# Moving the six weight conversions of the first attention stage one pair later, and holding ScalarE's first step of each in its place

## The chip, the cores and the metric

One core of one Trainium2 chip. The metric is the device time of one execution in microseconds (us), the median over runs. Engines by their short names: PE (TensorE, matrix products), PEld (its weight loads), ACT (ScalarE), DVE (VectorE), POOL (GpSimd), SP (SyncE, which issues the transfers here).

## The reference

Three stages of one network, all in float32:

```python
scores = q @ k.T / sqrt(64); scores[masked] = -1e9          # 4 x 12 heads, 448 x 64, causal
attn   = softmax(scores) @ v
x      = attn as (1792, 768)                                 # tokens by heads x width
h      = x @ w_in                                            # 768 x 2048, w_in is float64 in memory
x      = max(0.01 * h, h) @ w_out                            # 2048 x 768, float64 too
logits = x @ phi                                             # 32 slots
out    = softmax(logits, 1) @ experts(softmax(logits, 0).T @ x)   # 8 experts, w1 and w2
```

The float64 inputs of this step are turned into narrower numbers on the chip; that is what the text calls a conversion.

## The kernel before

**Attention** goes by pairs of heads: 6 pairs for each of the 4 batches, 24 in all, numbered n. It is a generator (L587) whose every step is called a slot, three slots to a pair. For n up to 6, slot 0 of pair n is `attend(n-1)` (the product with v, tile `O`), `lowering(n)` (tiles `mps`, `mr`) and `weights(n, 0)` (scores `T`, then the exponential into `P`); slot 1 is `inverses(n-1)` (tile `dn`, then a reciprocal `r` on DVE), maxima of pair n+1 (scores `S`, DVE's `junk`) and `weights(n, 1)`; slot 2 is `columns(n-1)` (tiles `rb`, `rs`, `x`), `weights(n, 2)`, more maxima and the transposes `qkps`, `qkt` of pair n+2. In `weights` POOL masks `P` (L481) and adds up `tsum` (L486, L490), which `inverses` reads.

**The first stage** (`stage(SLOTS * NP + LEAD, EARLY[0])`, L902) has 21 slots, numbered x: pairs 0 to 6 of attention, and in between six conversions of `w_in`, f = 0 to 5. The loop of `stage` (L873 to L882) takes one slot of attention, then `prep_step(BEFORE)`, then starts conversions that are due, then `prep_step(AFTER)`. Where they are due is a ramp: up to `ceil(6 * (x + 1) / 17)` are started by slot x, which gives slots 0, 2, 5, 8, 11, 14.

**A conversion** (`prep_in`, L242) has three parts. In its starting slot s (`to_f32`, L219): ACT takes the absolute value of the high words (L230, tile `cv_i`, `t` in the code), ACT takes their sign (L231, tile `cs_i`), DVE a maximum (`w_am`, L233), a shift (L234) and an or (L235) that puts the low words in; then `load_raw` issues the transfer that is due next into the freed buffer. At the end of slot s+1 `pow2_scale` (L137) makes a scale: one product on PE (`w_ps`) and short steps on DVE (`w_m`, `w_e`, `w_s`). In slot s+2 ACT scales the sign, POOL multiplies it in (L254), ACT copies the high half (`w`, L262; for f = 0 and 4 POOL does that, L260), POOL subtracts for the low half (L263). Raw tiles have 3 buffers, `cv_i` 4, `cs_i` 2 in this stage.

**The order of the work.** PE's products run in the order in which the program states them (`in_order`, L102). On the other engines a planner sets the order: it goes through a simulated time line and gives an engine whatever is ready by it, attention ahead by a priority offset (`AHEAD`, 300). `tc.issue_after(i)` holds an instruction behind i in its engine's queue, without waiting for i to finish. From the second stage on (`fixed[0] = True`, L910) ACT is in program order as well; in the first it is not. Transfers are all on SP's queue; the raw tiles are issued behind the last load of attention (`last_load`, L195).

**The second stage** begins with pair 7; from here PE also runs the large product `H` of the batch before (18 products for each of 16 columns of `w_in`), which needs all six `x` of its batch and the converted `w` of its column. Its own pool of raw tiles lies in the memory of the first stage's, which it gets tile by tile as that comes free.

Of the kernel before, what the change touches and what calls it, by code (L numbers as in the profile page):

```python
# [10 lines left out]
F32 = mybir.dt.float32  # L11
# [4 lines left out]
AF = mybir.ActivationFunctionType  # L16
# [18 lines left out]
def tile_attn_moe_softmoe(ctx: ExitStack, tc: tile.TileContext, q, k, v, w_in, w_out, phi, w1, w2, out, dbg=None):  # L35
# [60 lines left out]
    def last_on(engine):  # L96
        return next(i for i in reversed(nc.cur_bb.bb.instructions[-400:]) if i.engine == engine)
# [21 lines left out]
    scalar = Scalar()  # L119
# [56 lines left out]
    for x, u in enumerate(units):  # L176
        stage = 0 if x < EARLY[0] else 1 if x < whole else 2
        order += [u + (h, stage) for h in ((0, 1) if stage == 2 else (None,))]
# [5 lines left out]
    def load_raw():  # L184

        while waiting:
            u = waiting[0]
            kind, f, h, stage = u
            pool, n = pools[stage], BUFS[stage][0]
            if pool is None or sum(x[3] == stage for x in raws) == n:  # L190
                return
            waiting.pop(0)
            w = DM if h is None else DH
            t = pool.tile([128, w, 2], I32, tag="raw", bufs=n, name=f"raw_{kind}{f}_{h}")
            with tc.issue_after(last_load[0]):  # L195
                if kind == "i":
                    nc.sync.dma_start(
                        t.rearrange("p (c f) t -> p c (f t)", f=128),
                        w_in32[:, 256 * f : 256 * (f + 1)].rearrange("(c p) f -> p c f", p=128),
                    )  # L200
                else:
                    g0, ng = 2 * (h or 0), w // (DM // 4)
                    rows = w_out32[128 * f + 32 * g0 : 128 * f + 32 * (g0 + ng)].rearrange("(g p) c -> p g c", p=32)
                    for e in range(4):
                        with tc.issue_after(last_on(mybir.EngineType.SP)) if e else ExitStack():
                            nc.sync.dma_start(
                                t[32 * e : 32 * e + 32].rearrange("p (g c) t -> p g (c t)", g=ng),
                                rows[:, :, DM // 2 * e : DM // 2 * (e + 1)],
                            )
            raws[u] = t  # L210
# [8 lines left out]
    def to_f32(u, absmax=None):  # L219

        raw = raws.pop(u)
        kind, f, h, stage = u
        nm = f"{kind}{f}_{h}"
        w = DM if h is None else DH
        hw, lw = raw[..., 1], raw[..., 0]
        _, nt, ns = BUFS[stage]
        t = pools[stage].tile([128, w], F32, tag="cv_t", bufs=nt, name="cv_" + nm)
        sg = pools[stage].tile([128, w], BF16, tag="cv_s", bufs=ns, name="cs_" + nm)
        ti = t.bitcast(I32)
        scalar.activation(t, hw.bitcast(F32), AF.Abs, scale=2.0**-112)  # L230
        scalar.activation(sg, hw.bitcast(F32), AF.Sign)  # L231
        if absmax is not None:
            nc.vector.tensor_reduce(absmax, t, AX.X, ALU.max)  # L233
        nc.vector.tensor_scalar(ti, ti, 3, None, ALU.logical_shift_left)  # L234
        nc.vector.scalar_tensor_tensor(ti, lw, 29, ti, ALU.logical_shift_right, ALU.bitwise_or)  # L235
        load_raw()
        return t, sg
# [4 lines left out]
    def prep_in(u):  # L242

        f = u[1]
        am = const.tile([128, 1], F32, tag="w_am", bufs=2, name=f"w_am{f}")
        t, sg = to_f32(u, am)
        yield AFTER
        yield AFTER
        s_w, _ = pow2_scale(am, f"w{f}", 20, out=inv_w[:, f : f + 1])
        yield BEFORE  # L250
        if u[3]:
            yield BEFORE
        scalar.activation(sg, sg, AF.Copy, scale=s_w)
        nc.gpsimd.tensor_tensor(t, t, sg, ALU.mult)  # L254
        if u[3]:
            yield BEFORE
        w = t.rearrange("p (c f) -> p c f", c=NP)
        hi, lo = (w16[f][:, x] for x in range(2))
        if f < EARLY[0] and f % 4 < HIP:
            nc.gpsimd.tensor_copy(hi, w)  # L260
        else:
            scalar.copy(hi, w)  # L262
        nc.gpsimd.tensor_tensor(lo, w, hi, ALU.subtract)  # L263
        ready.add(u[:2])

    def prep_out(us):
# [5 lines left out]
        for u in us:  # L272
            wo, sg = to_f32(u)
            nc.gpsimd.tensor_tensor(wo, wo, sg, ALU.mult)  # L274
            wo = wo.rearrange("p (g c) -> p g c", c=DM // 4)
            g0, ng = 2 * (u[2] or 0), wo.shape[1]
            for e in range(4):
                with tc.issue_after(last_on(mybir.EngineType.SP)) if e else ExitStack():
                    nc.sync.dma_start(
                        rows[:, g0 : g0 + ng, DM // 4 * e : DM // 4 * (e + 1)], wo[32 * e : 32 * e + 32]  # L280
                    )
            wos.append((wo, g0, ng))
            if u is not us[-1]:
                yield BEFORE
# [27 lines left out]
    started = [0]  # L312
    running = []

    def prep_step(phase):

        for x in list(running):
            if x[1] == phase:
                x[1] = next(x[0], None)
                if x[1] is None:  # L320
                    running.remove(x)

    def prep_start():
        u = units[started[0]]
        started[0] += 1
        us = [x for x in order if x[:2] == u]
        g = prep_in(us[0]) if u[0] == "i" else prep_out(us)
        running.append([g, next(g)])
# [540 lines left out]
    def stage(slots, count, columns_of_g=None):  # L869

        had = started[0]
        last = slots - (6 if columns_of_g is not None and count <= NF else 4)
        for x in range(slots):  # L873
            with tc.high_priority(offset=AHEAD):
                next(slots_of_attention, None)
            prep_step(BEFORE)
            while started[0] < min(count, had + -(-(count - had) * (x + 1) // last)):
                prep_start()
            if columns_of_g is not None and x not in GAPS:
                with tc.high_priority(offset=AHEAD):  # L880
                    next(columns_of_g)
            prep_step(AFTER)  # L882
        if columns_of_g is not None:
            with tc.high_priority(offset=AHEAD):
                for _ in columns_of_g:
                    pass
        while running:
            prep_step(BEFORE)
            prep_step(AFTER)

    if True:
# [6 lines left out]
        for e in range(4):  # L898
            nc.sync.dma_start(
                phi_sb[32 * e : 32 * e + 32], phi[DM // 4 * e : DM // 4 * (e + 1)].rearrange("(y x) s -> x y s", x=32)  # L900
            )
        stage(SLOTS * NP + LEAD, EARLY[0])  # L902
        tc_release(pools[0])
        tc_release(psum)
# [6 lines left out]
        for b in range(1, 4):  # L911
            if b == 3:
                tc_release(pools[1])
                tc_release(ring[0])
                mainp = tc.alloc_tile_pool(name="mainp", bufs=1, reuse_waits="tile")
                ring[0] = tc.alloc_tile_pool(name="gring2", bufs=1, reuse_waits="tile")
                pools[2] = tc.alloc_tile_pool(name="conv", bufs=1, side="right", reuse_waits="tile")
                load_raw()
                g_nat = [mainp.tile([128, S // 64, DFF // 4], F32, name=f"g_nat{h}") for h in range(2)]
            stage(SLOTS * NP, sum(EARLY[: b + 1]) if b < 3 else 2 * NF, up(b - 1))  # L920
# [322 lines left out]
```

## Time and profile before

| what | value |
|---|---|
| median of 3 runs | 623.68 us (623.65 to 625.51) |
| the profiled execution, its time | 622.72 us |
| its span, first to last instruction | 621.0 us (1.7 us lie around it) |
| PE busy | 560.4 us, 90% |
| DVE busy | 399.7 us, 64% |
| ACT busy | 277.4 us, 45% |
| POOL busy | 240.7 us, 39% |
| mean granted clock of PE | 0.988 |

Times in the trace are microseconds from the start of the span. The time line lists, for one engine, groups of alike instructions: start, duration, engine, line, operation, tiles, count, and in brackets how long the engine had been idle and what it had waited for. Most of ACT's and PE's lines are those of a helper (L115, L104), so groups are told apart by their tiles. Buffer numbers are left out: `cv_i_None` is the tile of any of the conversions of this stage, and which f it is follows from the order.

### The profile page before, as it was taken

How to read it: one execution, taken by the hardware profiler on the slowest of the kernel's cores; microseconds unless marked ns; L12 is line 12 of the kernel's file. 1: busy time of each engine (PE TensorE's matmuls, PEld its weight loads, DVE VectorE, ACT ScalarE, POOL GpSimd, SP SyncE). 2: the span in 40 equal slices, each digit the busy share in tenths (PEclk: the TensorE clock that was granted, in tenths of full speed). 3: DMA queues.
4: the chain of work that ended last, by engine and by line, in shares of the span. 5: the costliest groups of instructions: out<-in, count | busy, mean ns of one | idle time of the engine just before them, and what ended most of it. 6: DMA issues, size and time to landing. Idle time of an engine off the chain costs nothing.

```text
span 621.0 us, 12409 instructions
## 1 busy us (share of the span) xinstructions
PE 560.4 (90%) x4720; PEld 316.4 (51%) x4720; DVE 399.7 (64%) x970; ACT 277.4 (45%) x538; POOL 240.7 (39%) x247
## 2 busy tenths in 40 slices
PE   4788888997999999899999999999999999996584
PEld 3455555654555555555555555554434444552353
DVE  5988657998984686898779999642866433001014
ACT  2577655678765466556445554431112121001013
POOL 5476973488686372576445443430000000000000
PEclk9989999998999999999999999999999999999998
DMA  9972337754783388895344323219959559999998
GB/s 182 275 166 46 68 74 206 216 155 116 174 179 88 74 213 198 196 201 127 110 109 96 109 78 90 58 60 319 366 223 421 196 210 392 426 417 427 402 334 301
DMA packets 137308, 125.70 MB, mean 202 GB/s; under 512 B 86688, under 2 KB 131232, under 8 KB 133792
## 3 DMA queue, kind: packets, MB, share of 16 engines
q1 hardware_dynamic: 137248, 124.91, 65.6%
q8 instruction: 37, 0.61, 0.4%
q14 instruction: 23, 0.19, 0.1%
HBM read 105.74 MB, written 19.14 MB: 201 GB/s over the span
## 4 chain that ended last, share of the span: by engine, by line
PE 56%; DMA 14%; DVE 10%; POOL 7%; issue 4%; ACT 4%; SPq 3%; DVEq 0%; ACTq 0%; POOLq 0%
PE H L104 26%; DMA w<-in_moe_w_dram 9%; PE O L104 5%; PE T L104 4%; PE g_acc L104 3%; PE dn L104 3%; PE L L104 3%; DMA raw_o_None<-in_moe_w_out_dram 2%; DVE rs L519 2%; PE S L104 2%; POOL w L263 2%; DVE junk L441 2%; DVE cv_i_None L235 2%; DMA raw_i_None<-in_moe_w_in_dram 1%; PE ph L1064 1%
## 5 line engine op out<-in xcount | busy, mean ns | idle before, releaser
L104 PE MATMUL H<-x,w 128*128 128x448 f16 x1152 | 229.9, 354 | 0.7 <-ACT g L115 0.7
L104 PEld LDWEIGHTS <-w 128*128 128x128 f16 x1152 | 110.3, 99 | 112.8 <-issue 19.6
L441 DVE CUSTOM_DVE_ANT_0 junk<-S,mask 112x224 bf16<-112x224 f32 (+3 forms) x192 | 84.1, 438 | 24.1 <-PE S L104 21.5
L115 ACT ACTIVATE P<-T 112x672 f32<-112x672 f32 (+1 forms) x72 | 57.0, 793 | 27.2 <-PE T L104 26.5
L519 DVE RECIPROCAL rs<-rs 128x224 f32<-128x224 f32 x36 | 53.2, 1519 | 19.1 <-ACT rs L115 19.0
L104 PE MATMUL T<-qkt 64*112 64x336 f32 (+3 forms) x576 | 60.6, 322 | 2.6 <-DVE mxe L441 2.5
L481 POOL TENSOR_SCALAR_AFFINE_SELECT P<-P 112x448 f32<-112x448 f32 x48 | 33.2, 695 | 75.8 <-ACT P L115 60.7
L115 ACT ACTIVATE g<-H,iv 128x448 f32<-128x448 f32 x48 | 30.5, 635 | 64.3 <-PE H L104 43.1
L104 PE MATMUL O<-P,v 112*64 112x448 f32 (+3 forms) x384 | 52.4, 413 | 4.5 <-POOL P L481 4.5
L104 PEld LDWEIGHTS T<-qkt 64*112 64x112 f32 x576 | 42.3, 179 | 17.7 <-issue 9.6
L490 POOL TENSOR_TENSOR tsum<-tsum,P 112x448 f32<-112x448 f32 (+1 forms) x48 | 49.4, 1029 | 1.9
L486 POOL TENSOR_TENSOR tsum<-P 112x672 f32<-112x672 f32 x24 | 39.8, 1658 | 1.7
L104 PEld LDWEIGHTS O<-P,v 112*64 112x64 f32 x384 | 25.4, 138 | 29.3 <-issue 12.3
L1056 POOL MEMSET hz<- 128x256 f32 x2 | 0.6, 312 | 100.9 <-PE pgt L104 100.3
L115 ACT ACTIVATE mr<-mps,own 128x112 fp32r<-128x112 f32 x96 | 26.2, 357 | 30.0 <-PE mps L104 30.0
L104 PE MATMUL S<-qkt 64*112 64x224 f32 (+3 forms) x192 | 31.3, 366 | 7.0 <-DVE mxe L441 2.6
L115 ACT ACTIVATE g_spare<-H,iv 128x448 f32<-128x448 f32 x16 | 10.2, 635 | 56.8 <-PE H L104 56.8
L104 PE MATMUL T<-mr,onesr 64*112 64x448 f32 (+1 forms) x192 | 30.6, 315 | 4.1 <-ACT mr L115 4.1
L254 POOL TENSOR_TENSOR cv_i_None<-cv_i_None,cs_i_None 128x768 f32<-128x768 f32 x16 | 28.6, 1786 | 10.5 <-ACT cs_i_None L115 10.5
L263 POOL TENSOR_TENSOR w<-cv_i_None,w 128x768 f16<-128x768 f32 x16 | 26.8, 1676 | 10.4 <-ACT w L115 10.3
L554 POOL TENSOR_TENSOR x<-rs,x 128x448 f16<-128x448 f32 x24 | 26.6, 1107 | 8.1 <-ACT x L115 8.1
L274 POOL TENSOR_TENSOR cv_o_None<-cv_o_None,cs_o_None 128x768 f32<-128x768 f32 x10 | 16.5, 1650 | 33.4 <-DVE cv_o_None L235 21.2
(180 smaller groups left out, 875.6 us busy)
## 6 DMA issues: line engine op xcount, KB each, us to landing
w<-in_moe_w_dram SPq DMA_DIRECT2D x30, 1536.0 KB, 14.6
raw_i_None<-in_moe_w_in_dram SPq DMA_DIRECT2D x16, 768.0 KB, 6.0
raw_o_None<-in_moe_w_out_dram SPq DMA_DIRECT2D x40, 192.0 KB, 4.4
g_far<-g SPq DMA_DIRECT2D x32, 224.0 KB, 2.3
gb<-g_far SPq DMA_DIRECT2D x8, 896.0 KB, 9.0
wo<-wsc SPq DMA_DIRECT2D x4, 1536.0 KB, 9.1
v<-in_v_dram SPq DMA_DIRECT2D x24, 224.0 KB, 4.3
out_dram<-ob SPq DMA_DIRECT2D x14, 384.0 KB, 3.8
```

The lines of the kernel that those rows point to most:

```text
L104: op(*args, **kwargs)
L115: op(*args, **kwargs)
L235: nc.vector.scalar_tensor_tensor(ti, lw, 29, ti, ALU.logical_shift_right, ALU.bitwise_or)
L254: nc.gpsimd.tensor_tensor(t, t, sg, ALU.mult)
L263: nc.gpsimd.tensor_tensor(lo, w, hi, ALU.subtract)
L274: nc.gpsimd.tensor_tensor(wo, wo, sg, ALU.mult)
L441: nc.vector.tensor_tensor_reduce(out=junk[:, :w], in0=ps[:, a, at : at + w], in1=mask[:, S - w :], scale=-1.0, scalar=3e38, op0=ALU.add, o ...
L481: nc.gpsimd.affine_select(out=d, in_=d, compare_op=ALU.is_ge, fill=0.0, base=0, pattern=[[0, 4], [1, CP]], channel_multiplier=-1,)
L486: nc.gpsimd.tensor_tensor(tsum[:CP], p[0][:CP, :, 0, CP:], p[0][:CP, :, 1, : S - CP], ALU.add)
L490: nc.gpsimd.tensor_tensor(y, y, p[1][:CP, :, j, : S - CP * (j + 2)], ALU.add)
L519: nc.vector.reciprocal(rs[:, c : c + S // 2], rs[:, c : c + S // 2])
L554: nc.gpsimd.tensor_tensor(x16[b][:, hp, 1], rs, hi, ALU.subtract)
```

## The change

In the first stage (`columns_of_g is None`) the ramp is replaced by a formula that starts conversions at slots 1, 5, 8, 11, 14 and 17. And in that stage, for f from 1 to 5, ACT's absolute value is held behind the ACT instruction that the program states last before it. The other stages keep their ramp.

```diff
@@ to_f32
-        scalar.activation(t, hw.bitcast(F32), AF.Abs, scale=2.0**-112)
+        with tc.issue_after(last_on(mybir.EngineType.Activation)) if stage == 0 and f else ExitStack():
+            scalar.activation(t, hw.bitcast(F32), AF.Abs, scale=2.0**-112)
         scalar.activation(sg, hw.bitcast(F32), AF.Sign)
@@ stage
-            while started[0] < min(count, had + -(-(count - had) * (x + 1) // last)):
+            if columns_of_g is None:
+                begun = min(x, 1) + max(x - 2, 0) // 3
+            else:
+                begun = had + -(-(count - had) * (x + 1) // last)
+            while started[0] < min(count, begun):
                 prep_start()
```

## Rows read from the trace of the kernel before

**Rows 1.** Busy time by stretch; its first line names the columns.
```profile
core 0: us, PE busy (x) PEld busy (x) DVE busy (x) ACT busy (x) POOL busy (x), PEclk, DMA share, GB/s
26.30:41.20 14.90, 12.19 (x102) 8.32 (x101) 14.41 (x43) 9.72 (x17) 11.01 (x9) 0.89 0.82 208
41.20:52.30 11.10, 9.60 (x102) 6.52 (x101) 8.91 (x30) 8.78 (x17) 8.65 (x9) 1.00 0.28 64
300.00:420.00 120.00, 116.89 (x887) 65.22 (x886) 92.13 (x204) 58.87 (x127) 54.06 (x55) 1.00 0.32 83
520.00:621.00 101.00, 77.57 (x842) 43.15 (x838) 15.08 (x41) 12.94 (x29) 2.84 (x16) 0.97 0.97 386
```

**Rows 2.** ACT's time line: start, length, engine, line, operation, tiles, count, [idle before].
```profile
20.05 0.89 ACT L115 ACTIVATE cv_i_None<-raw_i_None 128x768 f32<-128x768 f32 x1 [2.53 <-DMA raw_i_None<-in_moe_w_in_dram]
...
21.62 0.71 ACT L115 ACTIVATE P<-T 112x672 f32<-112x672 f32 x1
22.31 0.92 ACT L115 ACTIVATE cv_i_None<-raw_i_None 128x768 f32<-128x768 f32 x1
...
25.09 0.93 ACT L115 ACTIVATE cv_i_None<-raw_i_None 128x768 f32<-128x768 f32 x1 [1.05 <-DMA raw_i_None<-in_moe_w_in_dram]
25.92 0.70 ACT L115 ACTIVATE P<-T 112x672 f32<-112x672 f32 x1
```

**Rows 3.** Time line of PE, pairs 0 and 1.
```profile
21.98 0.80 PE L104 MATMUL w_ps<-ident,w_am 128*128 128x128 f32 x2 [2.95 <-DVE w_am L233]
...
24.25 0.48 PE L104 MATMUL S<-qkt 64*112 64x224 f32 x2
...
30.40 0.32 PE L104 MATMUL mps<-ident,mxe 112*128 112x112 f32 x1 [0.83 <-DVE mxe L441]
...
33.59 0.45 PE L104 MATMUL T<-mr,onesr 64*112 64x448 f32 x2 [1.88 <-ACT mr L115]
```

**Rows 4.** Time line of POOL, pairs 1 to 6.
```profile
37.96 0.58 POOL L481 TENSOR_SCALAR_AFFINE_SELECT P<-P 112x448 f32<-112x448 f32 x1 [3.11 <-ACT P L115]
...
49.12 0.60 POOL L481 TENSOR_SCALAR_AFFINE_SELECT P<-P 112x448 f32<-112x448 f32 x1 [2.37 <-ACT P L115]
...
55.64 1.65 POOL L263 TENSOR_TENSOR w<-cv_i_None,w 128x768 f16<-128x768 f32 x1
...
60.27 0.58 POOL L481 TENSOR_SCALAR_AFFINE_SELECT P<-P 112x448 f32<-112x448 f32 x1 [2.37 <-ACT P L115]
...
71.50 0.82 POOL L260 CAST w<-cv_i_None 128x768 f16<-128x768 f32 x1
...
95.54 0.58 POOL L481 TENSOR_SCALAR_AFFINE_SELECT P<-P 112x448 f32<-112x448 f32 x1 [4.70 <-ACT P L115]
...
99.44 1.88 POOL L490 TENSOR_TENSOR tsum<-tsum,P 112x448 f32<-112x448 f32 x2
```

**Rows 5.** Time line of PE, `dn` of pairs 2 and 6.
```profile
57.95 0.41 PE L104 MATMUL dn<-tsum,sixteen 128*64 128x112 f32 x4 [0.51 <-POOL tsum L490]
...
101.84 0.73 PE L104 MATMUL dn<-tsum,onesr 128*64 128x336 f32 x4
```

**Rows 6.** Time line of ACT: a sign in pair 2, the absolute value of f = 8.
```profile
53.81 0.92 ACT L115 ACTIVATE cs_i_None<-raw_i_None 128x768 bf16<-128x768 f32 x1
...
115.50 0.93 ACT L115 ACTIVATE cv_i_None<-raw_i_None 128x768 f32<-128x768 f32 x1
```

**Rows 7.** Time line of DVE, pairs 1 and 3.
```profile
30.26 2.18 DVE L235 SCALAR_TENSOR_TENSOR cv_i_None<-raw_i_None,cv_i_None 128x768 int32<-128x768 int32 x1
...
56.96 0.94 DVE L233 TENSOR_REDUCE w_am<-cv_i_None 128x1 f32<-128x768 f32 x1
...
58.55 0.85 DVE L529 RECIPROCAL r<-dn 128x112 f32<-128x112 f32 x1
59.31 0.90 DVE L235 SCALAR_TENSOR_TENSOR cv_i_None<-raw_i_None,cv_i_None 128x768 int32<-128x768 int32 x1
```

**Rows 8.** Time line of SP, the raw tiles of the second stage.
```profile
90.18 2.79 SPq L197 DMA_DIRECT2D raw_i_None<-in_moe_w_in_dram x3
```

## The prediction

> **What bounds the kernel now.** I read the busy times by stretch first, because the change touches only the first hundred microseconds. From pair 2 of the first stage a pair takes some 11 us, and PE is busy 9.60 of 11.10 at full clock; pair 1 takes 14.90, with 12.19 of PE at a mean clock of 0.89 [rows 1]. So pair 1 has about 4 us that the pairs behind it don't need. Much later, at 300 to 420 us, PE is busy 116.89 of 120: from there the kernel is a chain of products, and a lead that the first stage wins is carried along. The last stretch is full of transfers (DMA share 0.97), but those go into buffers that earlier work frees, so they move with it [rows 1]. I take the whole lead as carried.
>
> Then the time lines of the slow first pairs. On ACT, pair 0's second exponential (tile P) starts at 21.62, behind the absolute value of f = 0, which stood 2.53 us waiting for its transfer. Its third starts at 25.92, behind the absolute values of f = 1 and f = 2, and the latter waited 1.05 us for a landing [rows 2]. By the code these two belong to slots 2 and 5; the planner has drawn them forward, and ACT's queue holds the exponential behind them. PE shows what follows: 2.95 us idle ahead of w_ps, whose maximum DVE had not ready; the next scores S only at 24.25; 0.83 us ahead of mps at 30.40, since DVE still had parts of three conversions to do; and 1.88 us for ACT's mr at 33.59 [rows 3].
>
> Last, POOL for the steady part. It masks P of the pairs at 37.96, 49.12, 60.27 and so on; between the second and third lie 11.15 us, of which POOL is idle 2.37, so it works 8.8 [rows 4]. Its final sum releases dn, for which PE sat 0.51 us [rows 5]. A pair is therefore a loop: POOL's 8.8 us, then some 2.4 us over dn, the scores and the exponential back to POOL. A conversion is 3.3 us of it (two steps of 1.65 [rows 4]).
>
> **The change part by part.** No instruction is added or removed: six conversions move, and five absolute values are held in place.
>
> *Start.* The absolute values of f = 1 and 2 no longer stand ahead of the exponential. It is then bound by the one before it, which ends at 21.62 + 0.71 = 22.33 [rows 2]; the scores S, which need the buffer that this one frees, can start at about 22.4 instead of 24.25: 1.85 us [rows 2, 3]. w_ps of f = 0 moves to the end of slot 2, behind those scores, so PE's idle time ahead of it is part of the same gain. With two conversions gone from DVE and ACT here, the waits of 0.83 and 1.88 go too. Sum 4.56; I take 4.5. Bounds: 1.85 alone, if ACT and DVE stay as late as now; up to 7, if f = 0 too gets behind the exponential (2.53, [rows 2]). It isn't held by the change, so I leave it where it is, at no gain. What is late next is PE itself: pair 1 then has POOL work for f = 0 only, and PE's products set its length.
>
> *The loops from pair 2 to 5.* They now carry f = 1 to 4, one each, as before with other numbers. Before, four loops from 49.12 to 95.54 took 46.42 us, since the planner had drawn two conversions ahead of the mask [rows 4]. Held in place they should go like the one of 11.15, with POOL's copy for f = 4 (0.82, [rows 4]) in one of them: 4 x 11.15 + 0.82 = 45.4, a gain of 1.0. Bounds: 0, if they are drawn ahead again, and 1.8, if the copy falls into POOL's gap.
>
> *Holding the absolute value.* On ACT it should cost nothing: it comes where a sign of 0.92 stands now, at 53.81 [rows 6], and the sign, which is free, can go to where an absolute value of about 0.92 was [rows 2]. Without that exchange mr, behind it, would be 0.9 us late. On DVE it costs: the maximum (0.94), the shift and the or (0.90) of a conversion must now run between ACT's end at 54.7 and the reciprocal r of dn at 58.55, where attention's maxima run too; today the or comes behind r, at 59.31 [rows 6, 7]. Who waits for r is rb on PE, and all products behind it. From both sides: 0 if the planner leaves the or behind r, 0.90 a pair if it comes ahead [rows 7]. I take 0.35, nearer to the lower end, since attention has the better priority: 5 pairs x 0.35 = 1.7 lost.
>
> *The last conversion.* f = 5 moves from pair 5 to pair 6, where POOL now sits 4.70 us before its mask at 95.54 [rows 4]. But the conversion comes behind that mask: the sum of pair 6 ends at 99.44 + 1.88 = 101.32 and PE's dn comes at 101.84, a slack of 0.5 [rows 4, 5]. One step of 1.65 ahead of the sum costs 1.1 us, two cost 2.8; if both are put behind it, nothing. I take 1.4, near to one step.
>
> *Transfers.* The raw tiles of f = 3 to 5 are issued later, as their buffers free up, and have about a pair's time to land (the waits of [rows 2] are those for the first three, whose transfers the change does not touch). On SP the loads of q, k and v stand behind them, and those are due two pairs ahead. The raw tiles of the second stage go out at 90.18 [rows 8]; the third, that of f = 8, now needs memory that f = 5 holds until its last POOL step, near 100. Cover: the conversion of f = 8 begins at 115.50 [rows 6], 15 us later. I cost all this at nothing; without that cover it would be the few microseconds by which f = 5 is late.
>
> **The sum.** -4.5 - 1.0 + 1.7 + 1.4 = -2.4 us. The profiled execution took 622.72 (span 621.0 and 1.7 around it), which gives 620.3. The median of the runs is 0.96 above it, so the forecast of a median is 623.68 - 2.4 = **621.3 us**.
>
> **The rivals.** What a measurement of this kernel can tell from no change is about 0.3%, 1.9 us.
>
> *A, the forecast*: some -1 to -4.
>
> *B, the gain is kept whole.* f = 5 goes behind the sum into POOL's idle time, and DVE's or stays behind r: -4.5 - 1.0 = -5.5, and up to -7.5 if PE's clock also stays up in pair 1. About 618. For it: POOL has gaps in each pair [rows 4]. Against: DVE works 8.91 of 11.10 us in a pair [rows 1], and has to find room for three steps in a shorter stretch.
>
> *C, the change doesn't clear ACT.* Only the absolute value is held. The signs need the same raw tiles and are free; drawn forward to where the absolute values were, they keep the exponential behind a landing. Then the start gives its lower bound: -1.85 - 1.0 + 1.7 + 1.4 = +0.25, 624. For it: the planner fills ACT's idle time with anything ready. Against: there are two sign buffers, and the first stays taken until POOL has multiplied it.
>
> *D, slower: DVE in the first half of each pair.* The or comes ahead of r in pairs 2 to 6, and beside a busy POOL. In the trace the or takes 0.90 at 59.31, where POOL stands in its gap (the 2.37 us ahead of 60.27), and 2.18 at 30.26, where POOL works [rows 4, 7]. Between ACT's end and r POOL is at work, so it would cost between 0.90 and 2.18 a pair, say 1.5: 5 x 1.5 = 7.5 - 4.5 - 1.0 + 1.4 = +3.4, 627. It decides from (4.5 + 1.0 - 1.4) / 5 = 0.8 us a pair on. Against: attention's priority. The Trainium skill has a rule that bears on it: GPSIMD Engine Reference, 1. Specifications, says that POOL and DVE share their interfaces to the on-chip memory, and that DVE instructions with two such inputs contend; the or is one of them. By that rule the change is bad, as it moves these steps from POOL's gaps into its work; the trace agrees with 0.90 against 2.18.
>
> **How the numbers follow.** Chances: A 0.42, B 0.20, C 0.18, D 0.20. Faster by more than 0.3% (below 621.8) is B and somewhat over half of A, 0.48; within it the rest of A, most of C and the mild end of D, 0.32; slower the rest, 0.20. The range must reach into B and D: 617.5 (6.2 gained) to 626.5 (2.8 lost) leaves out the far ends of both, less than 0.2. A's own range is 620 to 622.7.
>
> **What would show it.** Right: on ACT no absolute value but that of f = 0 ahead of pair 0's third exponential, and that at about 22.4; POOL's mask of pair 1 at 33 to 34 instead of 37.96, of pair 2 near 45, of pair 6 near 91 to 92; dn of pair 6 at 99 to 100. A step fails if pair 1's mask is not 4 us earlier (start), if masks stand over 11.5 us apart from pair 2 on with r or w_ps awaited on PE (holding, D), or if PE waits 2 us or more for POOL's sum in pair 6 (last conversion). The forecast is wrong as a whole if the lead at the first H is over 2 us and the end is not earlier.

## The result, and the profile after

The changed kernel took **631.30 us** (median of 4 runs, 630.67 to 632.78) beside 624.11 for the one before (4 runs): a ratio of 1.0101, 95% interval 1.0079 to 1.0124 (ratios here and below are the recorded estimates, which differ a little from the quotient of the two medians, here 1.0115). It is slower by 1.0%; the forecast was 621.3, and even the upper end of its range, 626.5, lies 4.8 us below. The profiled execution took 630.67, its span is 628.9 against 621.0, the mean granted clock 0.977 against 0.988. Of the six conversions five moved by a pair, f = 0 by one slot. The work is the same: PE 565.4 us busy, DVE 401.5, ACT 276.6, POOL 240.6.

Where it went is seen at the head of each pair. Below stands when PE starts the product `O` of each pair (in slot 0 of the next one), in both traces, with the distance to the next:

| `O` of pair | before | distance | after | distance | after against before |
|---|---|---|---|---|---|
| 0 | 26.34 | 14.88 | 24.60 | 10.33 | -1.74 |
| 1 | 41.22 | 11.05 | 34.93 | 10.55 | -6.29 |
| 2 | 52.27 | 10.92 | 45.48 | 16.74 | -6.79 |
| 3 | 63.19 | 10.22 | 62.22 | 11.76 | -0.97 |
| 4 | 73.41 | 11.31 | 73.98 | 15.32 | +0.57 |
| 5 | 84.72 | 14.99 | 89.30 | 15.46 | +4.58 |
| 6 | 99.71 | | 104.76 | | +5.05 |
| first `H` | 102.66 | | 109.39 | | +6.73 |

By pair 3 the change is 6.8 us ahead, more than I had asked of the start. The next four pairs lose 11.8 us, and with another 1.7 behind `O` of pair 6, 6.7 us of loss are left at the first `H`. From there it is only carried: a block of `H` that starts at 480.34 before starts at 487.09 now.

The busy times by stretch, profile after (the answer to [rows 1]; the columns are the same):

```profile
24.60:34.90 10.30, 10.11 (x100) 6.72 (x99) 6.71 (x30) 5.67 (x12) 8.92 (x9) 1.00 0.79 169
34.90:45.50 10.60, 9.46 (x103) 6.35 (x101) 8.46 (x29) 6.89 (x14) 5.57 (x6) 1.00 0.53 141
45.50:62.20 16.70, 11.40 (x99) 7.71 (x99) 10.84 (x31) 10.08 (x19) 11.53 (x10) 0.86 0.35 90
62.20:74.00 11.80, 10.28 (x102) 6.71 (x101) 10.04 (x31) 7.13 (x14) 6.52 (x8) 0.91 0.26 58
74.00:89.30 15.30, 11.81 (x101) 8.03 (x100) 10.79 (x30) 8.85 (x17) 10.60 (x10) 0.78 0.21 47
89.30:104.80 15.50, 9.74 (x104) 6.55 (x103) 12.50 (x35) 8.49 (x17) 11.62 (x11) 1.00 0.32 73
300.00:420.00 120.00, 117.62 (x910) 66.10 (x908) 93.86 (x208) 59.83 (x130) 54.51 (x55) 1.00 0.34 87
```

Pair 1 was 14.90 us long with PE at 12.19 and a clock of 0.89; it is 10.30 long now with PE busy 10.11 at full clock. That is the gain. In pairs 3 to 5 PE stands still more often, and its mean granted clock falls to 0.86, 0.91 and 0.78, so a part of their time was run at the lower level of 1.2 GHz. (In pair 6, where PE is idle for 5.8 us, the clock is 1.00.) At 300 to 420 us the kernel is the chain of products that it was.

ACT's time line after, pair 0 first (answer to [rows 2]), then pairs 2 and 3:

```profile
19.64 0.89 ACT L115 ACTIVATE cv_i_None<-raw_i_None 128x768 f32<-128x768 f32 x1 [2.46 <-DMA raw_i_None<-in_moe_w_in_dram]
...
21.24 0.71 ACT L115 ACTIVATE P<-T 112x672 f32<-112x672 f32 x1
21.89 0.91 ACT L115 ACTIVATE cs_i_None<-raw_i_None 128x768 bf16<-128x768 f32 x1
22.71 0.71 ACT L115 ACTIVATE P<-T 112x672 f32<-112x672 f32 x1
...
42.23 0.94 ACT L115 ACTIVATE cs_i_None<-cs_i_None,w_s 128x768 bf16<-128x768 bf16 x1 [1.91 <-DVE w_s L148]
43.07 0.71 ACT L115 ACTIVATE P<-T 112x672 f32<-112x672 f32 x1
...
55.37 0.94 ACT L115 ACTIVATE cs_i_None<-cs_i_None,w_s 128x768 bf16<-128x768 bf16 x1 [0.39 <-DVE w_s L148]
58.06 0.83 ACT L115 CAST w<-cv_i_None 128x768 f16<-128x768 f32 x1 [1.75 <-POOL cv_i_None L255]
58.80 0.88 ACT L115 ACTIVATE cs_i_None<-raw_i_None 128x768 bf16<-128x768 f32 x1
59.59 0.71 ACT L115 ACTIVATE P<-T 112x672 f32<-112x672 f32 x1
```

In pair 0 no absolute value but that of f = 0 stands ahead of the third exponential, which starts at 22.71 instead of 25.92; one sign, that of f = 1, was drawn forward (21.89). In pair 2 ACT waits 1.91 us, and not for scores: the scaling of the sign (`cs` by `w_s`) is queued ahead of the second exponential and waits for DVE. In pair 3 the scaling, the copy `w` (which waits 1.75 us for POOL's multiply) and a sign are all queued ahead of it.

PE's time line after shows when the scores were there, and what came of it:

```profile
41.42 0.32 PE L104 MATMUL T<-mr,onesr 64*112 64x336 f32 x2
...
50.32 1.19 PE L104 MATMUL O<-P,v 112*64 112x224 f32 x8 [3.30 <-POOL P L482]
...
56.09 0.32 PE L104 MATMUL T<-mr,onesr 64*112 64x336 f32 x2
...
78.46 1.39 PE L104 MATMUL O<-P,v 112*64 112x224 f32 x8 [2.94 <-POOL P L482]
...
92.88 0.79 PE L104 MATMUL O<-P,v 112*64 112x224 f32 x8 [2.04 <-POOL P L482]
...
104.47 0.36 PE L104 MATMUL S<-qkt 64*112 64x224 f32 x2 [2.85 <-DVE qkt L420]
```

The scores of pair 2 are done at 41.74 (41.42 + 0.32), its exponential starts at 43.07: 1.3 us late. In pair 3 it is 56.41 against 59.59, 3.2 us. The second half of `O` then waits for `P`: 3.30 us in pair 2, 2.94 in pair 4, 2.04 in pair 5. The same product takes 0.79 us at 92.88, in a stretch with a granted clock of 1.00, and 1.39 at 78.46, in one of 0.78. The last line belongs to pair 6: there PE waits 2.85 us for `qkt`, and not for POOL.

POOL's time line after, pairs 1 to 3 (answer to [rows 4]):

```profile
32.49 0.58 POOL L482 TENSOR_SCALAR_AFFINE_SELECT P<-P 112x448 f32<-112x448 f32 x1 [0.88 <-ACT P L115]
...
43.24 1.66 POOL L255 TENSOR_TENSOR cv_i_None<-cv_i_None,cs_i_None 128x768 f32<-128x768 f32 x1 [4.71 <-ACT cs_i_None L115]
44.84 0.59 POOL L482 TENSOR_SCALAR_AFFINE_SELECT P<-P 112x448 f32<-112x448 f32 x1
...
47.10 1.64 POOL L264 TENSOR_TENSOR w<-cv_i_None,w 128x768 f16<-128x768 f32 x1
...
49.69 0.58 POOL L482 TENSOR_SCALAR_AFFINE_SELECT P<-P 112x448 f32<-112x448 f32 x1
...
60.57 0.58 POOL L482 TENSOR_SCALAR_AFFINE_SELECT P<-P 112x448 f32<-112x448 f32 x1
```

POOL follows ACT's order: the multiply goes ahead of the mask in pair 2, since its sign is ready before the exponential. POOL stood idle 4.71 us and then has everything to do at once; the second mask, for which `O` waits, starts only at 49.69. From the end of the scores to the start of the mask it is 3.1 us in pair 2 (41.74 to 44.84) and 4.2 in pair 3 (56.41 to 60.57). With nothing in between it is about one exponential (e11 below: exponential at 42.48, mask at 43.28).

Last, DVE in pair 2, after:

```profile
39.69 0.95 DVE L236 SCALAR_TENSOR_TENSOR cv_i_None<-raw_i_None,cv_i_None 128x768 int32<-128x768 int32 x1
40.56 0.28 DVE L143 TENSOR_REDUCE w_m<-w_ps 128x1 f32<-128x128 f32 x1
40.76 0.85 DVE L530 RECIPROCAL r<-dn 128x112 f32<-128x112 f32 x1
...
42.04 0.15 DVE L148 TENSOR_SCALAR w_s<-w_e 128x1 int32<-128x1 int32 x1
```

Shift and or belong here to the same conversion as the scale, f = 1 (its maximum ran at 37.27), and the or comes ahead of `w_m` and `r`. Before, conversions were drawn so far forward that the or beside a scale was that of a later one, and it came behind `r` [rows 7]. `r` itself is not late: PE's `dn` ends at 40.68. What is late in pair 2 is `w_s`, and with it the scaling that stands in the exponential's way; in pair 3 it is POOL's multiply, for which the copy ahead of the exponential waits. So two new orders act together, one on DVE and one on ACT. The runs below take them apart.

### The profile page after: what moved, and what is told of

Read it like the earlier page. It is cut to its first block, busy times and chain, and to the rows that moved or that the text cites. A ratio compares the mean times of both kernels' runs of the same rounds, so it can differ in the third digit from the quotient of the medians.

```text
span 628.9 us, 12407 instructions
## 1 busy us (share of the span) xinstructions
PE 565.4 (90%) x4720; PEld 317.5 (50%) x4720; DVE 401.5 (64%) x970; ACT 276.6 (44%) x538; POOL 240.6 (38%) x247
## 4 chain that ended last, share of the span: by engine, by line
PE 42%; DMA 9%; DVE 3%; ACT 1%; issue 1%; SPq 1%; DVEq 0%; ACTq 0%
PE H L104 21%; DMA w<-in_moe_w_dram 9%; PE g_acc L104 3%; PE T L104 3%; PE O L104 3%; PE L L104 3%; PE ph L1069 1%; PE dn L104 1%; DVE rs L520 1%; PE o L104 1%; PE S L104 1%; PE psi L1041 1%; PE wp_ps L104 1%; DVE junk L442 1%; PE po L104 1%
## 5 line engine op out<-in xcount | busy, mean ns | idle before, releaser
L104 PE MATMUL O<-P,v 112*64 112x448 f32 (+3 forms) x384 | 56.0, 434 | 8.6 <-POOL P L482 8.3
L104 PEld LDWEIGHTS O<-P,v 112*64 112x64 f32 x384 | 26.7, 145 | 35.5 <-issue 13.3
L264 POOL TENSOR_TENSOR w<-cv_i_None,w 128x768 f16<-128x768 f32 x16 | 26.8, 1674 | 11.4 <-ACT w L115 11.3
```

The source lines that it names most:

```text
L104: op(*args, **kwargs)
```

## The experiments

Each kernel was run beside the one before on the same chip. The expectations weigh three theories. **Q**: the loss comes from the order on ACT, where the scaling now stands ahead of the pair's second exponential, and with it POOL's multiply ahead of the mask. **S**: the later slots alone are to blame, above all the sixth conversion in pair 6. **D**: DVE has too much to do in the first half of a pair, as shift and or run ahead of `r` and `w_s`, beside a busy POOL. The table has every run, in us, with the medians of the kernel before in the same comparison.

| run | edit, in words | median | before | ratio (95%) |
|---|---|---|---|---|
| e1 | new slots, nothing held | 633.58 | 624.87 | 1.0128 (1.0087 to 1.0169) |
| e2 | old slots, absolute value held | 634.23 | 624.87 | 1.0146 (1.0122 to 1.0169) |
| e3 | the change, scaling held | 627.27 | 624.87 | 1.0036 (1.0020 to 1.0052) |
| e6 | the change, multiply held | 631.82 | 624.87 | 1.0101 (1.0080 to 1.0121) |
| e7 | e3, shift and or held too | 623.06 | 624.82 | 0.9965 (0.9938 to 0.9991) |
| e8 | e7 at the old slots | 624.66 | 624.82 | 0.9994 (0.9969 to 1.0018) |
| e5 | e3 at the old slots | 628.56 | 624.82 | 1.0043 (1.0016 to 1.0070) |
| e9 | e7, scaling of f = 0 free | 622.90 | 624.82 | 0.9965 (0.9937 to 0.9993) |
| e13 | the change, scaling held but for f = 0 | 624.72 | 624.73 | 0.9986 (0.9969 to 1.0003) |
| e12 | the change, shift and or held alone | 626.41 | 624.73 | 1.0026 (0.9999 to 1.0054) |
| e11 | e9, f = 5 behind attention in pair 6 | 620.50 | 624.73 | 0.9920 (0.9890 to 0.9951) |

### The two halves alone: e1 and e2

e1 is the changed kernel without the hold; e2 is the kernel before with it.

```diff
-        with tc.issue_after(last_on(mybir.EngineType.Activation)) if stage == 0 and f else ExitStack():
-            scalar.activation(t, hw.bitcast(F32), AF.Abs, scale=2.0**-112)
+        scalar.activation(t, hw.bitcast(F32), AF.Abs, scale=2.0**-112)
```

> The new slots without the holding of the absolute values. Theory Q (the loss comes from the order on ACT: the scaling of the sign, and with it POOL's multiply, gets ahead of the second exponential of its pair): the scaling stands ahead of it in pairs 2, 5 and 6 here and behind it in pairs 3 and 4, and the start has no gain, since absolute values stand ahead of the third exponential of pair 0 again; so 625 to 630 us, and mask to mask about 11 us between pairs 3 and 4, 12 or more elsewhere. Theory D (DVE has too much in the first half of a pair because the steps are held late): the steps are drawn ahead again, so at most 625. Theory S (the later slots alone are to blame, by the sixth conversion in pair 6): 630 to 632, as with the whole change.

> The old slots, with the absolute values held. Theory Q: the scaling stands ahead of the second exponential in pairs 1 to 5, and once the high half's copy too, so the loss is that of the whole change or more: 629 to 634. Theory D: the same side, 628 to 632, with the reciprocal of dn late on DVE. Theory S: no loss, 621 to 625.

Both medians lie above that of the whole change (633.58 and 634.23 against 631.30), though e1's interval overlaps the change's widely and e2's at its very end. In e1 the absolute value of f = 1 is back ahead of the third exponential, which starts at 24.22, and `O` of pair 1 at 39.28, 4.3 us behind the change; pairs 2 and 3 take 14.49 and 13.01. In e2 the gain of the start is absent too (`O` of pair 1 at 40.56), pair 3 takes 16.68. In e2 the third exponential comes at 26.69, behind a scaling and the absolute value of f = 1. So neither half clears the start alone: the 6.3 us at `O` of pair 1 need both. And both halves, each without the other, bring the scaling ahead of the exponential. ACT's time line of e1, pair 2:

```profile
48.09 0.94 ACT L115 ACTIVATE cs_i_None<-cs_i_None,w_s 128x768 bf16<-128x768 bf16 x1 [2.97 <-DVE w_s L148]
48.93 0.71 ACT L115 ACTIVATE P<-T 112x672 f32<-112x672 f32 x1
```

Q's order is there in both runs, but e1 is slower than Q had it (625 to 630). D, which had e1 at 625 at most, is contradicted by it as the only cause, and S, which had e2 without a loss, by e2. The order of the kernel before is one that any of these edits upsets.

### Holding the steps behind: e3 and e6

e3 holds the scaling behind ACT's last instruction before it in the program, e6 instead POOL's multiply behind POOL's.

```diff
-        scalar.activation(sg, sg, AF.Copy, scale=s_w)
+        with tc.issue_after(last_on(mybir.EngineType.Activation)) if u[3] == 0 else ExitStack():
+            scalar.activation(sg, sg, AF.Copy, scale=s_w)
```
```diff
-        nc.gpsimd.tensor_tensor(t, t, sg, ALU.mult)
+        with tc.issue_after(last_on(mybir.EngineType.Pool)) if u[3] == 0 else ExitStack():
+            nc.gpsimd.tensor_tensor(t, t, sg, ALU.mult)
```

> The whole change, and the scaling of the sign held behind the ACT instruction that the program states last before it, which is the second exponential of its pair. Theory Q: the steady pairs go back to some 11.2 us from mask to mask and the lead of 6 us that pair 2 has stays, less some 2 for the sixth conversion: 617 to 621. Theory D: DVE's steps stand where they stood, so nothing comes back: 629 to 632. Theory S: no change either, 629 to 632.

> The whole change, and POOL's multiply held behind the last POOL step before it (the sum of its pair's first exponential), while the scaling on ACT is free and still stands ahead of the second exponential. It tells the two halves of theory Q apart. If ACT's queue does the harm (the exponential waits for the scale from DVE): 627 to 631, with the second exponential still late. If POOL's queue does it (the mask waits for the multiply): 619 to 624.

e3 takes 4.0 us back, e6 nothing. With 627.27 e3 lies between Q's 617 to 621 and the 629 to 632 of the other two, so the scaling's place is a part of the loss and not the whole. In e6 the mask follows its exponential at once, but the exponential is queued behind the scaling as in the change. ACT's time line of e6, pair 2, and behind it POOL's:

```profile
43.06 0.94 ACT L115 ACTIVATE cs_i_None<-cs_i_None,w_s 128x768 bf16<-128x768 bf16 x1 [1.91 <-DVE w_s L148]
43.90 0.71 ACT L115 ACTIVATE P<-T 112x672 f32<-112x672 f32 x1
```
```profile
44.69 0.58 POOL L483 TENSOR_SCALAR_AFFINE_SELECT P<-P 112x448 f32<-112x448 f32 x1 [5.31 <-ACT P L115]
...
46.93 1.65 POOL L256 TENSOR_TENSOR cv_i_None<-cv_i_None,cs_i_None 128x768 f32<-128x768 f32 x1
```

POOL stands idle 5.31 us for the exponential, and only the multiply has gone behind. In this pair the harm is done in ACT's queue, and 631.82 is nearer to the 627 to 631 expected for that than to the 619 to 624 for POOL's.

### DVE's part: e7, e8, e5, e12, e13

e3 was still slower than the kernel before. In its pair 2 DVE's or takes 1.78 us, and POOL's final sum beside it 2.78 (1.88 in [rows 4]). DVE's line of e3, and behind it POOL's:

```profile
39.39 1.78 DVE L236 SCALAR_TENSOR_TENSOR cv_i_None<-raw_i_None,cv_i_None 128x768 int32<-128x768 int32 x1
```
```profile
38.91 2.78 POOL L492 TENSOR_TENSOR tsum<-tsum,P 112x448 f32<-112x448 f32 x2
```

e7 moves shift and or (and the issue of the transfer behind them) to the next slot, behind the steps that make the scale:

```diff
+        def rest():
+            held = stage == 0 and f
+            with tc.issue_after(last_on(mybir.EngineType.DVE)) if held else ExitStack():
+                nc.vector.tensor_scalar(ti, ti, 3, None, ALU.logical_shift_left)
+            nc.vector.scalar_tensor_tensor(ti, lw, 29, ti, ALU.logical_shift_right, ALU.bitwise_or)
+            load_raw()
...
+        if f in later:
+            later.pop(f)()
```

> The change with the scaling held, as in the run e3_scale_held, and DVE's shift and or of a conversion held behind its scale. In e3_scale_held pair 2 took 14.2 us from product O to product O: the or ran 1.78 us beside a busy POOL, POOL's sum beside it 2.78, and attention's maxima came behind both. Theory D in its second form (the shift and the or in the first half of a pair cost what is left of the loss): pairs 2 to 5 go to 10.5 to 11.5 us, 622 to 624.5. If they cost nothing: 626 to 628, as without.

> The old slots with all three holds (absolute value, scaling, shift and or). Against e9_first_free it tells what the slots alone are worth once nothing is drawn ahead. The slots were moved so that pair 1 carries one conversion instead of two; if that is worth what pair 1 shows (some 4 us) and the sixth conversion in pair 6 costs less than that, this is the slower of the two: 622 to 626. If the sixth conversion costs more than pair 1 gains, it is the faster: 618 to 621.

> The old slots with absolute value and scaling held, DVE's shift and or free. Against e3_scale_held it differs by the slots alone. Theory S in a weak form (the sixth conversion in pair 6 costs 3 us of the 17.7 that this pair takes in e3_scale_held): 623 to 625. If the slots don't matter: 626 to 628. Against e8_or_held_old it shows the shift and or a second time: 2 to 3 us above it by theory D, level with it otherwise.

With the three holds the change is at 623.06, below the kernel before (the interval ends at 0.9991); pairs 1 to 5 take 10.8 to 11.4 us each. At the old slots the same holds give 624.66. Without the hold of shift and or, the old slots stand at 628.56: this hold is worth some 4 us at either set of slots (627.27 to 623.06, 628.56 to 624.66), as long as the scaling of f = 0 is held too. What the new slots add under equal holds, 623.06 against 624.66, is within the two intervals and not shown.

e12 and e13 hold one of the two alone, beside e9, which holds both (in e9 and e13 the scaling of f = 0 is left free; pair 1's mask stands at 34.74 in e7 and at 32.45 in e9). Holding that scaling too costs 2.5 us where shift and or are free (e3 against e13): it puts POOL's low half of f = 0 at 37.30 in e3, beside the shift of f = 1, and the sum behind it beside the or. Where they are held, e7 and e9 are level.

> The change, and DVE's shift and or held behind the conversion's scale; the scaling on ACT is free and stands ahead of the second exponential in pairs 2 to 6, once the copy too. Theory Q (the order on ACT and POOL does most of the harm): 627 to 631. Theory D (DVE's shift and or do): 622 to 625.

> The change, and the scaling of f = 1 to 5 held behind the second exponential of its pair; the first conversion's scaling and DVE's shift and or are as in the change. Theory Q: most comes back, 622 to 626. Theory D: 628 to 631. Beside e9_first_free (622.9) it gives the price of the shift and or with everything else in its place: theory D in its weak form says 2 to 3 us, and pair 2 at 12 to 14 us as in e3_scale_held.

> As e7_or_held, but the first conversion's scaling is free, as in the change itself, so that POOL is through with it ahead of pair 1's mask. Theory Q with D: pair 1's mask stays at 32.5, pairs 2 to 5 take 10.5 to 11.5 us, pair 6 keeps some 2 to 3 us for the sixth conversion: 619 to 622, at or below the kernel before. If clock and slots hold it up anyway: 625 or more.

From 631.30, the scaling held gives 624.72 (-6.6), shift and or held 626.41 (-4.9), both 622.90 (-8.4): less than the sum of 11.5, so the two overlap. With the scaling held, shift and or are worth 1.8 more (e13 to e9, with intervals that overlap); with them held, the scaling 3.5 (e12 to e9). Q's range for e13 was met, its 627 to 631 for e12 was not, and neither of D's was; e9 lies 0.9 above the 622 that was expected at most. ACT in e12, pair 2, shows the overlap:

```profile
42.35 0.94 ACT L115 ACTIVATE cs_i_None<-cs_i_None,w_s 128x768 bf16<-128x768 bf16 x1 [0.38 <-DVE w_s L148]
43.44 0.73 ACT L115 ACTIVATE P<-T 112x672 f32<-112x672 f32 x1
```

The scaling is still ahead of the exponential, but with the or out of the way `w_s` is there 0.38 us after ACT asks for it, not 1.91; pairs 1 to 5 take 11.2 to 11.6 us, 0.5 to 0.8 more than in e9. In these pairs the wrong order on ACT costs little, since what it waits for is early. In e13 the order on ACT is right and DVE's is not; besides pair 6, the third pair is long, 13.97. DVE's time line there, and behind it POOL's:

```profile
49.53 2.07 DVE L235 TENSOR_SCALAR cv_i_None<-cv_i_None 128x768 int32<-128x768 int32 x1
```

```profile
49.54 1.63 POOL L265 TENSOR_TENSOR w<-cv_i_None,w 128x768 f16<-128x768 f32 x1
```

In e11 the same step runs where POOL stands idle:

```profile
42.21 0.50 DVE L239 TENSOR_SCALAR cv_i_None<-cv_i_None 128x768 int32<-128x768 int32 x1
```

The shift takes 0.50 us there. In e13 it starts beside a POOL step of 1.63 and lasts 2.07. A maximum, the or and the steps of the scale are queued behind it, so that `r` starts at 53.69, 1.1 us after the end of `dn`.

### The last conversion: e11

In e9 pair 6 alone is still long, 16.69 us at a granted clock of 0.78. There POOL makes the low half of f = 5 (`w`, at 92.97) ahead of the second mask. e11 states the copy and the low half of f = 5 one slot later and holds them behind attention's ACT and POOL steps of that pair:

```diff
+        if f == EARLY[0] - 1:
+            yield BEFORE
...
-            scalar.copy(hi, w)
-        nc.gpsimd.tensor_tensor(lo, w, hi, ALU.subtract)
+            with tc.issue_after(last_on(mybir.EngineType.Activation)) if f == EARLY[0] - 1 else ExitStack():
+                scalar.copy(hi, w)
+        with tc.issue_after(last_on(mybir.EngineType.Pool)) if f == EARLY[0] - 1 else ExitStack():
+            nc.gpsimd.tensor_tensor(lo, w, hi, ALU.subtract)
```

> As e9_first_free, and the last conversion's copy and low half held one slot longer and behind ACT's and POOL's steps of pair 6. In e9_first_free pairs 6 and 7 take 16.69 and 20.1 us against 14.99 and 18.67 before. If the sixth conversion's place in pair 6 is what costs these 3 us: pair 6 at some 13 to 15, the first H at 96 to 98 instead of 100.0, and 618 to 621 us. If something else holds pair 6 up (the clock, the loads): 622 to 624, as e9_first_free.

The profile of e11: POOL's time line in pair 6, ACT's in pair 2, and busy times of pair 6, of its second part (from `rb` on) and of the stretch from `O` of pair 6 to the first `H`:

```profile
93.72 0.58 POOL L500 TENSOR_SCALAR_AFFINE_SELECT P<-P 112x448 f32<-112x448 f32 x1
94.39 1.87 POOL L509 TENSOR_TENSOR tsum<-tsum,P 112x448 f32<-112x448 f32 x2
96.22 1.64 POOL L282 TENSOR_TENSOR w<-cv_i_None,w 128x768 f16<-128x768 f32 x1
```

```profile
42.48 0.73 ACT L115 ACTIVATE P<-T 112x672 f32<-112x672 f32 x1 [1.47 <-PE T L104]
43.10 0.93 ACT L115 ACTIVATE cs_i_None<-cs_i_None,w_s 128x768 bf16<-128x768 bf16 x1
```

```profile
79.70:94.40 14.70, 10.03 (x104) 6.54 (x103) 12.02 (x35) 8.51 (x16) 12.17 (x13) 1.00 0.26 59
88.80:92.80 4.00, 3.06 (x42) 2.52 (x42) 2.91 (x13) 2.96 (x7) 3.83 (x4) 1.00 0.00 0
94.40:99.00 4.60, 4.60 (x28) 2.20 (x27) 1.07 (x6) 0.00 (x0) 3.38 (x3) 0.63 0.95 256
```

The second part of pair 6 in e9, and PE's wait at its end:

```profile
88.00:92.00 4.00, 3.92 (x37) 3.37 (x38) 2.46 (x11) 1.99 (x4) 3.78 (x4) 0.54 0.00 0
```
```profile
95.17 0.53 PE L104 MATMUL S<-qkt 64*112 64x224 f32 x2 [1.90 <-DVE qkt L434]
```

In e11 the exponential waits for its scores alone and the scaling follows it; the low half follows the sum. Pair 6 takes 14.67 us at a clock of 1.00; the first `H` comes at 98.99, where 96 to 98 was expected. At 620.50 this version beats both kernels: 0.8% below the one before, where the change alone is 1.0% above. PE's order is that of the change, no work is added and none left out.

How much of the step from e9 to e11 the hold brings is open. The intervals of the two overlap, and in e9 the granted clock is at 0.54 from 88.00 to 92.00 already, before the moved steps run (the copy at 92.05, the low half at 92.97) and behind waits of PE like those of e11 (1.22 and 0.72 us, 1.21 and 0.79). From `rb` to the end of `qkps` the same products take 5.26 us in e9 and 3.63 in e11.

## Why the prediction was wrong

**The start (-4.5): right in mechanism and near in size.** Pair 1's mask comes at 32.49 (forecast 33 to 34, before 37.96), the third exponential at 22.71 (22.4). At that mask the gain is 5.5, one above the sum. It takes both halves: `O` of pair 1 comes at 39.28 in e1, at 40.56 in e2 and at 34.93 here, 41.22 before. Rival C is out: a sign was drawn forward as it feared, but its transfer had landed and it cost 0.8 us.

**The loops ("held in place they should go like the one of 11.15", -1.0): this step failed.** They took 16.74, 11.76, 15.32 and 15.46 us from `O` to `O` for pairs 3 to 6. From mask to mask, as the forecast counts, the four take 55.96 (44.84 to 100.80) against 45.4 in the forecast and 46.42 before: 9.5 lost in place of 1.0 gained. I held the planner's order of pairs 2 and 3 for a property of the pair. It was a result of the conversions drawn forward. ACT's time line before, pair 2, and behind it DVE's:

```profile
48.32 0.73 ACT L115 ACTIVATE P<-T 112x672 f32<-112x672 f32 x1 [1.17 <-PE T L104]
49.38 0.94 ACT L115 ACTIVATE cs_i_None<-cs_i_None,w_s 128x768 bf16<-128x768 bf16 x1 [0.33 <-DVE w_s L148]
```
```profile
49.21 0.14 DVE L148 TENSOR_SCALAR w_s<-w_e 128x1 int32<-128x1 int32 x1
```

With a later conversion's maximum, shift and or, and `r`, between `w_m` (45.84) and `w_s` (49.21), the scale came behind the exponential. In the changed kernel the scaling stands ahead of it. Why the planner's time line has the scaling ready first is argued from this order, not shown; that its place, with a late `w_s`, does harm is shown by e3 and e13.

**Holding (+1.7): the order that I gave a fifth of the chance came, on another path.** The sentence that failed is "I take 0.35, nearer to the lower end, since attention has the better priority". The or goes ahead of `r` in pair 2 and takes 0.95 to 1.77 us in pairs 2 to 6. Rival D had this order and priced it at 1.5 a pair for `r`. But `r` was hardly late (40.76 behind a `dn` that ends at 40.68 in pair 2, and at most 1 us in the pairs behind); it was `w_s`, then the scaling, the exponential and the mask. My price looked only at DVE's first waiter. I followed what the held instruction delays, and not what the conversion's next steps do on each queue once it sits elsewhere. The hold of shift and or gives back 4.9 us (e12), against 1.7 in the sum; with the scaling held as well, 1.8 of that is left (e13 to e9). Of the Trainium skill's rule (GPSIMD Engine Reference, 1. Specifications) that POOL and DVE share interfaces, these runs show a size: the or from 0.89 to 2.96 (e2, at 29.89, beside POOL steps of 1.46 and 1.63), the shift from 0.50 to 2.82 (e5, at 41.98), POOL's sum from 1.88 to 2.78 (e3). The side that D took, slower, was the right one, but in part by luck: its 627 was too mild, and its path through `r` has no place for ACT.

**The last conversion (+1.4): this path failed too.** I priced a POOL step ahead of POOL's sum, with PE waiting for the sum. In pair 6 PE waits for `qkt` instead: 2.85 us in the change, 1.90 in e9, 1.60 in e11, 1.18 before. The cast that makes `qkt` is queued on ACT behind the last exponential, and in e9 the copy of f = 5, which waits for POOL's multiply, holds that exponential to 92.78; ACT is free from 91.44 on. The lower clock holds `qkps`, which the cast reads, to 93.27. Either alone would have held the cast back (an estimate from these rows): it starts 14.47 us after `O` of pair 5 in e9, 12.61 in e11. So the copy is a term that the sum lacks, and what it is worth apart from the clock is not shown; the time fell by 2.4 us from e9 to e11, pair 6 from 16.69 to 14.67.

**Transfers (nothing): held.** In pairs 1 to 6 ACT waits for no raw tile in the profile after. The absolute value of f = 8 comes at 122.22 instead of 115.50, later by the same 6.7 us as `H`.

**Carried to the end: held, with the other sign.** 6.7 at the first `H`, 6.75 in the block near 480, 7.2 in the medians. My sign for holding and D, "masks over 11.5 us apart from pair 2 on", was met: 32.49, 44.84 and 60.57 in the profile after. But what was awaited was `P`, not `r` or `w_ps`.

From pair 1's mask to the first `H` the sum gave back 2.1 us of the gain (-1.0 + 1.7 + 1.4); it was 12.2. The gain of 5.5 to 6.8 at the start was real, and some 8.4 were lost to the two new orders in the planner's queues (e9). e9, without these, is 5.8 us ahead of the kernel before at `O` of pair 5 and 2.6 at the first `H`: 3.2 us go in pair 6 and behind it, at mean clocks of 0.78 and 0.66 where the kernel before has 0.89 and 1.00. e11 loses 1.7 there, between `O` of pair 6 and the first `H` (4.63 us at a clock of 0.63, 2.95 at 1.00 before). How much of e11's 4.2 us below the kernel before comes from the later slots is not shown: it was not run at the old ones, and e7 and e8 leave the slots' worth open.

## What to carry to other kernels

Where a planner sets the order of a queue, holding or moving one instruction re-orders everything behind it. Before such an edit is costed at the instruction that it names, list for each engine what the moved chain issues next, and which instruction of the critical loop would stand behind it; then hold those steps too, or expect them ahead. A wait whose releaser is not on the critical loop (here ACT ahead of the exponential, waiting for a weight's scale) is the sign to look for.

## What the runs showed that was not expected

A DVE shift with one input took 0.50 us beside an idle POOL and 2.07 beside a busy one; I had priced the or alone, which has two inputs. In e13 it starts at 49.53 and ends at 51.60, and POOL's step that starts with it ends at 51.17: what is left behind that end, 0.43, is about the shift alone. The Trainium skill (SBUF — State Buffer, Who interferes with whom) says that such a one-input step can take the shared ports too, and that the later of the two engines then stands until the other's instruction is done; the length of this row agrees with it. Which of the two issued first can't be read here: the shift's record starts 0.01 us ahead of POOL's.

The two halves of the change cost 1.3% and 1.5% alone and 1.0% together: their losses don't add up.
